# Batch 0 attended partly in front of the feed-forward and partly inside it, casts on GpSimd, weights cast by their transfers: windowed attention and a gated feed-forward in one kernel

## The chip, the cores and the metric

The kernel runs on one core of a Trainium2 chip. The metric is the device time of one execution in microseconds (us); lower is better. The engines are TensorE (PE, with its weight loads as PEld), VectorE (DVE), ScalarE (ACT), GpSimd (POOL) and SyncE (SP), which issues all transfers of the kernel before.

## What is computed

```python
# q, k, v: (B, H, S, D) = (4, 8, 768, 64) float32; n_sink = 4, window = 128
scores = q @ k^T / sqrt(D)
keep = (key position < 4) | (0 <= query position - key position < 128)
a = softmax over keys of the kept scores
x = (a @ v), heads side by side: (3072, 512)
out = (max(x @ w_gate, 0) * (x @ w_val)) @ w_out     # w_gate, w_val: 512 x 1536; w_out: 1536 x 512
```

## The kernel before

A *unit* is two heads of one batch; `U` holds 16 units, four to a batch (`NP` = 4). Its work is a row of six *stages*: `T(u)` transposes k and q on PE and copies them out of PSUM into `kE` (ACT) and `qT` (DVE); `Sg(u, g)`, for g = 0 to 2, makes the scores of a group of key blocks on PE and their exp on ACT into `ee`; `V(u, part)`, for two halves of the sequence, multiplies by v and by ones on PE and divides on DVE (two 32x32 transposes, a reciprocal, a product) into `xT`. The mask comes in one of two ways: with `bias=True` a matmul adds it (L199), otherwise DVE multiplies the exp by `msk` (L209).

Ahead of the stages stand the loads on SP's queue, `load_kq` (L89) and `load_v` (L94), and the casts from float32 to bf16, `cast_qk` (L110) and `cast_v` (L103). `cast_v` also copies the first four rows of v into three places (L108).

The feed-forward runs in *chunks*: `chunk(b, g, m)` (L235) makes 128 of the 1,536 hidden columns (m of 12) for half g of batch b: four matmuls with `wg` (L242), relu on ACT (L245), four with `wv` (L247), a product on DVE into `hT` (L249). It needs `xT` of all four units of the batch for its half. `ffn2(b, t, m)` (L256) is the second layer, 12 matmuls for each 128 rows, then a copy on ACT and a store from SP.

The order is written out by hand, and each engine and queue takes its instructions in the order of the program. Batch 0 is attended first, all four units with their three groups and both halves (L285 to L306). The weights come through a float32 staging buffer `wst` and are cast on GpSimd (L114 to L131, called from L291 to L312). Then 96 *slots* follow, one chunk each, 24 to a batch; in the slots of a batch the stages of the next batch's units are placed:

```python
slots = [(0, g, m) for m in range(FM) for g in range(2)]
...
want.append(max(0, s - 11) * 2)                      # slots 0 to 23: stages placed after slot s
...
want.append(min(len(stages), 24 + (s - 23)))         # later slots: one stage each
```

So the 24 stages of batch 1 lie in slots 12 to 23, two to a slot, and from slot 24 on each slot holds one stage. From slot 24 on up to three `ffn2` matmuls are taken in each slot from a queue (L356). Units 4 to 6 are loaded before the slots, a later unit three units ahead, when its forerunner's T comes (L317).

PSUM: `PP` is a pair of two-bank tiles that T, Sg and V take in turn; inside the slots T takes both, one for k and one for q (L177). `G` are four single banks; a chunk takes two of the first three in rotation.

Of the kernel before, what the change touches and what calls it, by code (L numbers as in the profile page):

```python
# [19 lines left out]
def kernel(  # L20
# [28 lines left out]
    NQ, NV, NW, NE, NT = 3, 3, 3, 3, 3  # L49
# [9 lines left out]
    wst = [const.tile([128, 2048], F32, name=f"wst{i}") for i in range(NW)]  # L59
# [43 lines left out]
    def cast_v(u, eng):  # L103
        src, dst = vf[u.i % NV], vn[u.i % NV]
        eng.tensor_copy(dst[:].rearrange("p j h d -> p (j h d)"), src[:].rearrange("p j h d -> p (j h d)"))  # L105
        o = dst[0:4, 1:7, :, :].rearrange("p (i e) h d -> p i e (h d)", e=2)[:, :, 0, :]
        s = src[0:4, 0, :, :].rearrange("p h d -> p (h d)").unsqueeze(1).to_broadcast([4, 3, 128])
        eng.tensor_copy(o, s)  # L108

    def cast_qk(u, ke, qe):  # L110
        for eng, src, dst in ((ke, kf[u.i % NQ], kn[u.i % 2]), (qe, qf[u.i % NQ], qn[u.i % 2])):
            eng.tensor_copy(dst[0:PR], src[0:PR].rearrange("p h (n d) -> p n h d", d=64))  # L112

    def load_w(c, w, dst, i, o):  # L114
        n = 256
        nc.sync.dma_start(out=wst[i % NW][:, o:o + KO * n].rearrange("p (ko n) -> p ko n", n=n),
                          in_=w.rearrange("(ko ki) n -> ki ko n", ki=128)[:, :, c * n:(c + 1) * n])

    def cast_w(c, dst, i, o, eng):
        n = 256  # L120
        eng.tensor_copy(dst[:, :, c * n:(c + 1) * n],
                        wst[i % NW][:, o:o + KO * n].rearrange("p (ko n) -> p ko n", n=n))

    def load_wo(c, i):
        nc.sync.dma_start(out=wst[i % NW][:].rearrange("p (ko n) -> p ko n", n=d_model),
                          in_=moe_w_out.rearrange("(ko ki) n -> ki ko n", ki=128)[:, 4 * c:4 * c + 4, :])

    def cast_wo(c, i, eng):
        for h in range(2):
            eng.tensor_copy(wo[:, 4 * c + 2 * h:4 * c + 2 * h + 2, :].rearrange("p ko n -> p (ko n)"),  # L130
                            wst[i % NW][:, 1024 * h:1024 * h + 1024])  # L131
# [137 lines left out]
    with tc.manual_schedule():  # L269
        for i in range(NV):  # L270
            nc.vector.memset(vf[i][:, 6, :, :], 0.0)
        for u in U[0:3]:
            load_kq(u)
            if u.p:
                load_v(U[u.p - 1])
        setup()

        def head_T(u):
            cast_qk(u, nc.gpsimd, nc.vector)
            T(u)  # L280

        head_T(U[0])
        load_kq(U[3])
        load_v(U[2])
        for p in range(NP):  # L285
            if p + 1 < NP:
                head_T(U[p + 1])
            for g in range(3):
                Sg(U[p], g, bias=True)
            cast_v(U[p], nc.gpsimd)  # L290
            if p == 0:  # L291
                load_v(U[3])
                for c in range(3):
                    load_w(c, moe_w_gate, wg, c, 0)
                    load_w(c, moe_w_val, wv, c, 1024)
            if p >= 1:
                for part in range(2):
                    V(U[p - 1], part)
        for c in range(6):
            cast_w(c, wg, c, 0, nc.gpsimd)  # L300
            cast_w(c, wv, c, 1024, nc.gpsimd)
            if c + 3 < 6:
                load_w(c + 3, moe_w_gate, wg, c + 3, 0)
                load_w(c + 3, moe_w_val, wv, c + 3, 1024)
        for part in range(2):
            V(U[3], part)  # L306
        for u in U[4:7]:
            load_kq(u)
            load_v(u)
        for c in range(3):  # L310
            load_wo(c, c)
            cast_wo(c, c, nc.gpsimd)  # L312

        head[0] = False
        stages = []

        def first(i):  # L317
            cast_qk(U[i], nc.gpsimd, nc.gpsimd)
            cast_v(U[i], nc.gpsimd)
            T(U[i])  # L320
            if i + 3 < len(U):
                load_kq(U[i + 3])
                load_v(U[i + 3])

        def stage_T(i):
            return lambda: first(i)

        n_u = len(U)
        order = []
        for i in range(NP, n_u):  # L330
            order.append(stage_T(i))
            order += [lambda i=i, g=g: Sg(U[i], g) for g in range(3)]
            order += [lambda i=i, part=part: V(U[i], part) for part in range(2)]

        stages = order
        slots = [(0, g, m) for m in range(FM) for g in range(2)]
        for b in range(1, B):
            slots += [(b, g, m) for g in range(2) for m in range(FM)]
        want = []
        for s in range(len(slots)):  # L340
            if s < 24:
                want.append(max(0, s - 11) * 2)
            else:
                want.append(min(len(stages), 24 + (s - 23)))
        f2 = deque()
        si = 0
        for s, (b, g, m) in enumerate(slots):
            if s % 24 == 0:
                while si < min(len(stages), 24 * b):
                    stages[si]()  # L350
                    si += 1
            chunk(b, g, m)
            while si < want[s]:
                stages[si]()
                si += 1
# [46 lines left out]
```

## Time and profile before

| | us |
|---|---|
| median of 3 runs | 309.78 (308.88 to 309.84) |
| the profiled execution | 308.14 |
| its span in the profile | 306.4 |

The span is what the profile covers from its first to its last instruction; 1.74 us of the profiled execution lie around it. A page cuts the span into 40 slices of 7.66 us and gives each engine's busy share in tenths. Times in the rows are counted from the span's start. "Idle before" is the time in which the engine had nothing to do before the instruction, with what ended it.

### The profile page before, as it was taken

The numbers are of one execution on the slowest core, as the hardware profiler recorded it, in microseconds if no ns is written. First come the engines' busy times: TensorE is split into PE (matmuls) and PEld (weight loads), VectorE is DVE, ScalarE is ACT, GpSimd is POOL, SyncE is SP. The second block draws the span as 40 slices with busy tenths as digits, with TensorE's granted clock in tenths as the row PEclk, the third lists the DMA queues.
The fourth block names the chain that finished last, engine by engine and source line by source line (L and its number), as shares of the span: only waits on it lengthen the run. The fifth ranks groups of instructions, "written<-read, shape, count | busy, mean of one in ns | idle before, by whom it ended". The sixth has DMA issues, their size and how long they took to land.

```text
span 306.4 us, 5389 instructions
## 1 busy us (share of the span) xinstructions
PE 264.9 (86%) x2114; PEld 147.6 (48%) x2136; DVE 160.2 (52%) x300; ACT 123.6 (40%) x250; POOL 72.7 (24%) x90
## 2 busy tenths in 40 slices
PE   1868659908796977999999999999999999999995
PEld 1343435504444544555555555555555555555442
DVE  5453953403947767575757575757575622222100
ACT  3464303304343453545454545454535233333221
POOL 5457640189424044040404040400000000000000
PEclk9995989965958999999999999999999999999999
DMA  7999999939972300150446044000000000000022
GB/s 197 241 249 348 349 253 230 335 128 232 233 162 69 89 0 2 51 141 37 130 104 148 37 127 99 0 36 34 37 0 36 34 36 34 35 36 34 34 103 103
DMA packets 44104, 35.13 MB, mean 115 GB/s; under 512 B 27184, under 2 KB 33328, under 8 KB 44080
## 3 DMA queue, kind: packets, MB, share of 16 engines
q1 hardware_dynamic: 44080, 34.81, 43.8%
q8 instruction: 16, 0.26, 0.4%
q14 instruction: 8, 0.07, 0.1%
HBM read 28.51 MB, written 6.29 MB: 114 GB/s over the span
## 4 chain that ended last, share of the span: by engine, by line
PE 71%; DVE 10%; DMA 8%; SPq 3%; ACT 2%; issue 2%; POOL 2%; DVEq 0%; ACTq 0%; POOLq 0%
PE g L262 18%; PE g L242 17%; PE g L247 17%; PE pp L203 5%; PE pp L220 4%; PE pp L262 3%; DMA wst<-in_moe_w_out_dram 3%; DMA vf<-in_v_dram 3%; PE pp L180 2%; PE pp L199 2%; DMA qf<-in_q_dram 2%; ACT ee L207 2%; DVE R L228 2%; DVE xT L230 2%; DVE t L226 2%
## 5 line engine op out<-in xcount | busy, mean ns | idle before, releaser
L249 DVE TENSOR_TENSOR hT<-gs,g 128x384 bf16<-128x384 f32 x96 | 53.1, 553 | 68.2 <-PE g L247 67.3
L245 ACT ACTIVATE gs<-g 128x384 f32<-128x384 f32 x96 | 47.2, 491 | 98.4 <-PE g L242 88.3
L242 PE MATMUL g<-xT,wg 128*128 128x384 bf16 x384 | 82.2, 338 | 4.1 <-DVE xT L230 4.1
L247 PE MATMUL g<-xT,wv 128*128 128x384 bf16 x384 | 81.6, 337 | 0.0
L262 PE MATMUL g<-wo,hT 128*128 128x512 bf16 x218 | 61.0, 381 | 1.6 <-issue 0.6
L207 ACT ACTIVATE ee<-pp 128x1006 bf16<-128x1006 f32 (+2 forms) x48 | 45.4, 959 | 32.6 <-PE pp L203 32.5
L242 PEld LDWEIGHTS <-wg 128*128 128x128 bf16 x384 | 37.4, 100 | 37.4 <-issue 6.9
L247 PEld LDWEIGHTS <-wv 128*128 128x128 bf16 x384 | 38.8, 101 | 28.6 <-issue 5.2
L209 DVE TENSOR_TENSOR ee<-ee,msk 128x1006 bf16<-128x1006 bf16 (+2 forms) x36 | 25.2, 703 | 26.9 <-ACT ee L207 26.7
L112 POOL CAST kn<-kf 96x1024 bf16<-96x1024 f32 x16 | 16.6, 1036 | 89.9 <-PE pp L180 62.4
L262 PEld LDWEIGHTS <-hT 128*128 128x128 bf16 x288 | 24.5, 98 | 24.8 <-issue 3.3
L203 PE MATMUL pp<-qT,kE 64*128 64x251 bf16 (+4 forms) x224 | 20.1, 282 | 4.6 <-DVE qT L185 4.6
L228 DVE STREAM_TRANSPOSE R<-r 128x384 f32<-128x384 f32 x32 | 18.5, 579 | 1.1
L203 PEld LDWEIGHTS <-kE 64*128 64x128 bf16 x224 | 8.1, 100 | 22.5 <-issue 17.2
L266 ACT COPY ot<-g 128x512 f32<-128x512 f32 x20 | 11.7, 583 | 15.8 <-PE g L262 15.8
L220 PEld LDWEIGHTS <-vn 128*64 128x64 bf16 x288 | 12.8, 110 | 10.0 <-issue 8.9
L105 POOL CAST vn<-vf 128x896 bf16<-128x896 f32 x16 | 15.0, 940 | 8.6 <-DMA vf<-in_v_dram 8.6
L180 PEld LDWEIGHTS <-kn 96*128 96x128 bf16 x128 | 7.9, 107 | 18.9 <-POOL kn L112 14.8
L185 DVE COPY qT<-pp 128x768 bf16<-128x768 bf16 x12 | 11.5, 957 | 9.6 <-PE pp L180 8.7
L226 DVE STREAM_TRANSPOSE t<-pp 128x384 f32<-128x384 f32 x24 | 13.9, 579 | 2.5 <-PE pp L220 1.7
L230 DVE TENSOR_TENSOR xT<-pp,R 128x384 bf16<-128x384 f32 x24 | 13.4, 557 | 0.8
L180 PE MATMUL pp<-ident,kn 96*128 96x96 bf16 x96 | 6.4, 211 | 8.1 <-POOL kn L112 7.5
(55 smaller groups left out, 183.5 us busy)
## 6 DMA issues: line engine op xcount, KB each, us to landing
kf<-in_k_dram SPq DMA_DIRECT2D x16, 384.0 KB
qf<-in_q_dram SPq DMA_DIRECT2D x16, 384.0 KB
vf<-in_v_dram SPq DMA_DIRECT2D x32, 192.0 KB
out_dram<-ot SPq DMA_DIRECT2D x24, 256.0 KB
wst<-in_moe_w_gate_dram SPq DMA_DIRECT2D x6, 512.0 KB
wst<-in_moe_w_val_dram SPq DMA_DIRECT2D x6, 512.0 KB
wst<-in_moe_w_out_dram SPq DMA_DIRECT2D x3, 1024.0 KB
vf<-in_v_dram SPq DMA_DIRECT2D x16, 12.0 KB
```

The source lines that it names most:

```text
L180: nc.tensor.transpose(ps.bitcast(BF16)[:, 96 * n:96 * n + 96], x[0:PR, n, :, :].rearrange("p h d -> p (h d)"), ident[0:PR, 0:PR])
L203: nc.tensor.matmul(out=ps[:, h, c0:c1], lhsT=kE[t][64 * h:64 * h + 64, x0:x0 + 128], rhs=qT[t][64 * h:64 * h + 64, q0:q0 + c1 - c0], start ...
L207: nc.scalar.activation(x, ps[:, :, 0:n], Act.Exp, bias=0.0, scale=scale)
L209: nc.vector.tensor_tensor(x, x, msk[:, g, 0:n].unsqueeze(1).to_broadcast([128, 2, n]), op=Alu.mult)
L220: nc.tensor.matmul(out=(pv, pd)[which][64 * h:64 * h + 64, o0:o0 + c1 - c0], lhsT=w, rhs=ee[u.i % NE][:, g, h, c0:c1], start=i == 0, stop= ...
L226: nc.vector.transpose(out=t1[:], in_=pd[:, 0:CUT])
L228: nc.vector.transpose(out=R[:].rearrange("p (c e) -> p c e", e=32), in_=r[:].unsqueeze(2).to_broadcast([128, CUT // 32, 32]))
L242: nc.tensor.matmul(out=gp[:, 0:CUT], lhsT=wg[:, ko, m * 128:(m + 1) * 128], rhs=x[:, ko, c], start=ko == 0, stop=ko == KO - 1)
L245: nc.scalar.activation(gs[:], gp[:, 0:CUT], Act.Relu, bias=0.0, scale=1.0)
L247: nc.tensor.matmul(out=vp[:, 0:CUT], lhsT=wv[:, ko, m * 128:(m + 1) * 128], rhs=x[:, ko, c], start=ko == 0, stop=ko == KO - 1)
L249: nc.vector.tensor_tensor(h[:, m, c], gs[:], vp[:, 0:CUT], op=Alu.mult)
L262: nc.tensor.matmul(out=op, lhsT=hT[b % 2][:, m, t * 128:(t + 1) * 128], rhs=wo[:, m, :], start=m == 0, stop=m == FM - 1)
```

## The change

The order of batch 0 is new. Before the slots stand T of its four units, the first two score groups and the first V half of each, and the third group of units 0 and 1. The rest (the third group of units 2 and 3, the second V half of each) goes into slots 0 to 5, one stage to a slot. Slots 0 to 5 are chunks 0 to 5 of the first half, slots 6 to 11 the same chunks of the second half, and then the halves alternate as before. The 24 stages of batch 1 lie in slots 6 to 23, four to three slots; from slot 24 on everything stands in the slots of before.

`T` no longer brings its casts along: `front(i)` issues casts and loads four slots ahead of T, and loads one unit ahead. All casts of q and k are on GpSimd; the row copies of `cast_v` are on ACT for batch 0. `gate(u)` writes two elements of the unit's `kf` on GpSimd, so that SP's load of that unit waits until GpSimd's queue has come to that point.

The staging buffer and its casts are gone. `load_w(m0, m1)` and `load_wo(c)` are transfers that GpSimd issues and that convert from float32 to bf16 on the way, eight for `wg` and `wv` (two of 256 columns and two of 512 for each) and three for `wo`. `kE`, `qT`, `ee`, `vf` and `vn` get four buffers instead of three.

```diff
--- before.py
+++ after.py
@@ -46,7 +46,7 @@
     npool = ctx.enter_context(tc.tile_pool(name="np", bufs=2))
     pspool = ctx.enter_context(tc.tile_pool(name="ps", bufs=1, space=bass.MemoryType.PSUM))
 
-    NQ, NV, NW, NE, NT = 3, 3, 3, 3, 3
+    NQ, NV, NE, NT = 3, 4, 4, 4
     kf = [const.tile([128, 2, 512], F32, name=f"kf{i}") for i in range(NQ)]
     qf = [const.tile([128, 2, 512], F32, name=f"qf{i}") for i in range(NQ)]
     vf = [const.tile([128, 7, 2, 64], F32, name=f"vf{i}") for i in range(NV)]
@@ -56,7 +56,6 @@
     ee = [const.tile([128, 3, 2, 512], BF16, name=f"ee{i}") for i in range(NE)]
     qn = [const.tile([128, NR, 2, 64], BF16, name=f"qn{i}") for i in range(2)]
     kn = [const.tile([128, NR, 2, 64], BF16, name=f"kn{i}") for i in range(2)]
-    wst = [const.tile([128, 2048], F32, name=f"wst{i}") for i in range(NW)]
     wg = const.tile([128, KO, d_ff], BF16, name="wg")
     wv = const.tile([128, KO, d_ff], BF16, name="wv")
     wo = const.tile([128, FM, d_model], BF16, name="wo")
@@ -100,35 +99,28 @@
         nc.sync.dma_start(out=dst[0:24, 6, :, :],
                           in_=v[u.b, 2 * u.p:2 * u.p + 2, 744:768, :].rearrange("h s d -> s h d"))
 
-    def cast_v(u, eng):
+    def cast_v(u, sinks):
         src, dst = vf[u.i % NV], vn[u.i % NV]
-        eng.tensor_copy(dst[:].rearrange("p j h d -> p (j h d)"), src[:].rearrange("p j h d -> p (j h d)"))
+        nc.gpsimd.tensor_copy(dst[:].rearrange("p j h d -> p (j h d)"), src[:].rearrange("p j h d -> p (j h d)"))
         o = dst[0:4, 1:7, :, :].rearrange("p (i e) h d -> p i e (h d)", e=2)[:, :, 0, :]
-        s = src[0:4, 0, :, :].rearrange("p h d -> p (h d)").unsqueeze(1).to_broadcast([4, 3, 128])
-        eng.tensor_copy(o, s)
-
-    def cast_qk(u, ke, qe):
-        for eng, src, dst in ((ke, kf[u.i % NQ], kn[u.i % 2]), (qe, qf[u.i % NQ], qn[u.i % 2])):
-            eng.tensor_copy(dst[0:PR], src[0:PR].rearrange("p h (n d) -> p n h d", d=64))
-
-    def load_w(c, w, dst, i, o):
-        n = 256
-        nc.sync.dma_start(out=wst[i % NW][:, o:o + KO * n].rearrange("p (ko n) -> p ko n", n=n),
-                          in_=w.rearrange("(ko ki) n -> ki ko n", ki=128)[:, :, c * n:(c + 1) * n])
-
-    def cast_w(c, dst, i, o, eng):
-        n = 256
-        eng.tensor_copy(dst[:, :, c * n:(c + 1) * n],
-                        wst[i % NW][:, o:o + KO * n].rearrange("p (ko n) -> p ko n", n=n))
-
-    def load_wo(c, i):
-        nc.sync.dma_start(out=wst[i % NW][:].rearrange("p (ko n) -> p ko n", n=d_model),
-                          in_=moe_w_out.rearrange("(ko ki) n -> ki ko n", ki=128)[:, 4 * c:4 * c + 4, :])
-
-    def cast_wo(c, i, eng):
-        for h in range(2):
-            eng.tensor_copy(wo[:, 4 * c + 2 * h:4 * c + 2 * h + 2, :].rearrange("p ko n -> p (ko n)"),
-                            wst[i % NW][:, 1024 * h:1024 * h + 1024])
+        sinks(o, src[0:4, 0, :, :].rearrange("p h d -> p (h d)").unsqueeze(1).to_broadcast([4, 3, 128]))
+
+    def cast_kq(u):
+        for src, dst in ((kf[u.i % NQ], kn[u.i % 2]), (qf[u.i % NQ], qn[u.i % 2])):
+            nc.gpsimd.tensor_copy(dst[0:PR], src[0:PR].rearrange("p h (n d) -> p n h d", d=64))
+
+    def gate(u):
+
+        nc.gpsimd.memset(kf[u.i % NQ][0:1, 0, 0:2], 0.0)
+
+    def load_w(m0, m1):
+        for w, dst in ((moe_w_gate, wg), (moe_w_val, wv)):
+            nc.gpsimd.dma_start(out=dst[:, :, m0 * 128:m1 * 128],
+                                in_=w.rearrange("(ko ki) n -> ki ko n", ki=128)[:, :, m0 * 128:m1 * 128])
+
+    def load_wo(c):
+        nc.gpsimd.dma_start(out=wo[:, 4 * c:4 * c + 4, :],
+                            in_=moe_w_out.rearrange("(ko ki) n -> ki ko n", ki=128)[:, 4 * c:4 * c + 4, :])
 
     def setup():
         nc.vector.memset(warm[:], 0.0)
@@ -269,98 +261,108 @@
     with tc.manual_schedule():
         for i in range(NV):
             nc.vector.memset(vf[i][:, 6, :, :], 0.0)
-        for u in U[0:3]:
-            load_kq(u)
-            if u.p:
-                load_v(U[u.p - 1])
+        for i, what in ((0, load_kq), (1, load_kq), (2, load_kq), (0, load_v)):
+            what(U[i])
         setup()
-
-        def head_T(u):
-            cast_qk(u, nc.gpsimd, nc.vector)
-            T(u)
-
-        head_T(U[0])
+        gp_copy, act_copy = nc.gpsimd.tensor_copy, nc.scalar.copy
+        cast_kq(U[0])
+        T(U[0])
+        cast_kq(U[1])
+        T(U[1])
         load_kq(U[3])
-        load_v(U[2])
-        for p in range(NP):
-            if p + 1 < NP:
-                head_T(U[p + 1])
-            for g in range(3):
-                Sg(U[p], g, bias=True)
-            cast_v(U[p], nc.gpsimd)
-            if p == 0:
-                load_v(U[3])
+        for u in U[1:4]:
+            load_v(u)
+        Sg(U[0], 0, bias=True)
+        cast_kq(U[2])
+        Sg(U[0], 1, bias=True)
+        cast_v(U[0], act_copy)
+        T(U[2])
+        Sg(U[1], 0, bias=True)
+        cast_kq(U[3])
+        Sg(U[1], 1, bias=True)
+        load_w(0, 2)
+        V(U[0], 0)
+        cast_v(U[1], act_copy)
+        T(U[3])
+        load_w(2, 4)
+        Sg(U[2], 0, bias=True)
+        Sg(U[2], 1, bias=True)
+        V(U[1], 0)
+        cast_v(U[2], act_copy)
+        gate(U[4])
+        load_kq(U[4])
+        load_v(U[4])
+        Sg(U[3], 0, bias=True)
+        Sg(U[3], 1, bias=True)
+        V(U[2], 0)
+        cast_v(U[3], act_copy)
+        load_w(4, 8)
+        Sg(U[0], 2, bias=True)
+        V(U[3], 0)
+        Sg(U[1], 2, bias=True)
+        head[0] = False
+
+        def prep(i):
+            cast_kq(U[i])
+            cast_v(U[i], gp_copy)
+
+        def load(i):
+            if i < len(U):
+                load_kq(U[i])
+                load_v(U[i])
+
+        def front(i):
+
+            prep(i)
+            if i == 4:
+                gate(U[5])
+                load(5)
+                load_w(8, 12)
+            elif i == 5:
+                gate(U[6])
+                load(6)
                 for c in range(3):
-                    load_w(c, moe_w_gate, wg, c, 0)
-                    load_w(c, moe_w_val, wv, c, 1024)
-            if p >= 1:
-                for part in range(2):
-                    V(U[p - 1], part)
-        for c in range(6):
-            cast_w(c, wg, c, 0, nc.gpsimd)
-            cast_w(c, wv, c, 1024, nc.gpsimd)
-            if c + 3 < 6:
-                load_w(c + 3, moe_w_gate, wg, c + 3, 0)
-                load_w(c + 3, moe_w_val, wv, c + 3, 1024)
-        for part in range(2):
-            V(U[3], part)
-        for u in U[4:7]:
-            load_kq(u)
-            load_v(u)
-        for c in range(3):
-            load_wo(c, c)
-            cast_wo(c, c, nc.gpsimd)
-
-        head[0] = False
-        stages = []
-
-        def first(i):
-            cast_qk(U[i], nc.gpsimd, nc.gpsimd)
-            cast_v(U[i], nc.gpsimd)
-            T(U[i])
-            if i + 3 < len(U):
-                load_kq(U[i + 3])
-                load_v(U[i + 3])
-
-        def stage_T(i):
-            return lambda: first(i)
-
-        n_u = len(U)
-        order = []
-        for i in range(NP, n_u):
-            order.append(stage_T(i))
-            order += [lambda i=i, g=g: Sg(U[i], g) for g in range(3)]
-            order += [lambda i=i, part=part: V(U[i], part) for part in range(2)]
-
-        stages = order
-        slots = [(0, g, m) for m in range(FM) for g in range(2)]
+                    load_wo(c)
+            else:
+                load(i + 1)
+
+        f2 = deque()
+        slots = [(0, 0, m) for m in range(6)] + [(0, 1, m) for m in range(6)]
+        slots += [(0, g, m) for m in range(6, FM) for g in range(2)]
         for b in range(1, B):
             slots += [(b, g, m) for g in range(2) for m in range(FM)]
-        want = []
-        for s in range(len(slots)):
-            if s < 24:
-                want.append(max(0, s - 11) * 2)
-            else:
-                want.append(min(len(stages), 24 + (s - 23)))
-        f2 = deque()
-        si = 0
+        plan = [[] for _ in slots]
+        first = [("V", 0, 1), ("S", 2, 2), ("V", 1, 1), ("S", 3, 2), ("V", 2, 1), ("V", 3, 1)]
+        for s, x in enumerate(first):
+            plan[s].append(x)
+        later = []
+        for i in range(NP, len(U)):
+            later += [("T", i, 0)] + [("S", i, g) for g in range(3)] + [("V", i, 0), ("V", i, 1)]
+        for x, st in enumerate(later):
+            plan[6 + x * 18 // 24 if x < 24 else x].append(st)
+        pre = [[] for _ in slots]
+        for s, p in enumerate(plan):
+            for st in p:
+                if st[0] == "T":
+                    pre[max(0, s - 4)].append(st[1])
         for s, (b, g, m) in enumerate(slots):
-            if s % 24 == 0:
-                while si < min(len(stages), 24 * b):
-                    stages[si]()
-                    si += 1
+            for i in pre[s]:
+                front(i)
             chunk(b, g, m)
-            while si < want[s]:
-                stages[si]()
-                si += 1
+            for what, i, x in plan[s]:
+                if what == "T":
+                    T(U[i])
+                elif what == "S":
+                    Sg(U[i], x, bias=i < NP)
+                else:
+                    V(U[i], x)
             for _ in range(3):
                 if f2:
                     f2.popleft()()
-            if b == 0 and s == 23:
+            if s == 23:
                 f2 += [lambda t=t, mm=mm: ffn2(0, t, mm) for t in range(6) for mm in range(FM)]
             if b > 0 and m == FM - 1:
                 f2 += [lambda b=b, t=t, mm=mm: ffn2(b, t, mm) for t in range(3 * g, 3 * g + 3) for mm in range(FM)]
-        assert si == len(stages)
         tail[0] = 1
         while f2:
             f2.popleft()()
```

## Rows read from the trace of the kernel before

**Rows 1.** The page: PE's busy tenths in 40 slices, and the transfer queue.
```profile
PE   1868659908796977999999999999999999999995
...
q1 hardware_dynamic: 44080, 34.81, 43.8%
```

**Rows 2.** Busy time by stretch (first line: the columns).
```profile
core 0: us, PE busy (x) PEld busy (x) DVE busy (x) ACT busy (x) POOL busy (x), PEclk, DMA share, GB/s
0.00:42.36 42.36, 25.12 (x289) 14.09 (x290) 25.11 (x60) 16.99 (x34) 24.21 (x35) 0.92 1.08 277
61.10:68.61 7.51, 0.00 (x0) 0.01 (x1) 0.55 (x1) 0.00 (x0) 6.26 (x8) 0.66 0.38 139
81.39:94.29 12.90, 10.28 (x91) 5.67 (x90) 8.30 (x16) 5.30 (x11) 3.44 (x4) 0.74 0.73 146
106.39:119.96 13.57, 9.18 (x108) 5.92 (x109) 10.73 (x21) 6.18 (x16) 4.89 (x6) 1.00 0.01 1
119.96:306.40 186.44, 181.20 (x1345) 99.83 (x1364) 93.28 (x167) 78.26 (x154) 18.93 (x23) 1.00 0.20 60
```

**Rows 3.** Timeline: start, duration, engine, instruction; in brackets the idle time before it.
```profile
14.30 0.69 DVE L112 CAST qn<-qf 96x1024 bf16<-96x1024 f32 x1 [2.39 <-DMA qf<-in_q_dram]
...
23.98 1.16 POOL L105 CAST vn<-vf 128x896 bf16<-128x896 f32 x1 [1.55 <-DMA vf<-in_v_dram]
...
42.36 0.81 PE L242 MATMUL g<-xT,wg 128*128 128x384 bf16 x4 [3.02 <-DVE xT L230]
...
108.35 0.50 PE L180 MATMUL pp<-ident,qn 96*128 96x96 bf16 x8 [1.46 <-DVE xT L230]
...
110.00 0.39 PE L203 MATMUL pp<-qT,kE 64*128 64x255 bf16 x4 [1.14 <-DVE qT L185]
```

**Rows 4.** Waits: total us, times, longest.
```profile
POOL wo L130 <- DMA wst<-in_moe_w_out_dram: 17.3, 3, 16.1
```

**Rows 5.** The chain that ended last: start, duration, what.
```profile
72.16 1.39 PE g L242 x4
...
124.12 0.75 PE g L262 x3
...
128.52 0.71 PE pp L220 x16
...
130.63 0.65 PE g L247 x4
131.28 0.83 PE pp L220 x20
...
143.89 0.71 PE pp L220 x16
```

**Rows 6.** Timeline of DVE, one unit and one mask product earlier.
```profile
73.24 1.12 DVE L209 TENSOR_TENSOR ee<-ee,msk 128x1006 bf16<-128x1006 bf16 x1 [1.83 <-ACT ee L207]
...
108.89 0.96 DVE L185 COPY qT<-pp 128x768 bf16<-128x768 bf16 x1
...
111.47 0.69 DVE L209 TENSOR_TENSOR ee<-ee,msk 128x1006 bf16<-128x1006 bf16 x1 [1.62 <-ACT ee L207]
...
114.45 0.55 DVE L249 TENSOR_TENSOR hT<-gs,g 128x384 bf16<-128x384 f32 x1
114.92 0.58 DVE L226 STREAM_TRANSPOSE t<-pp 128x384 f32<-128x384 f32 x1
...
116.88 0.57 DVE L226 STREAM_TRANSPOSE t<-pp 128x384 f32<-128x384 f32 x1
```

**Rows 7.** Groups by line: busy us, mean ns of one, idle before.
```profile
L207 ACT ACTIVATE ee<-pp 128x1006 bf16<-128x1006 f32 (+2 forms) x48 | 45.4, 959 | 32.6 <-PE pp L203 32.5
...
L112 POOL CAST qn<-qf 96x1024 bf16<-96x1024 f32 x12 | 12.4, 1032 | 2.9 <-PE pp L180 1.8 <-DMA vf<-in_v_dram 0.9
...
L108 POOL CAST vn<-vf 4x384 bf16<-4x384 f32 x16 | 8.6, 539 | 1.0
...
L112 DVE CAST qn<-qf 96x1024 bf16<-96x1024 f32 x4 | 2.7, 685 | 2.7 <-DMA qf<-in_q_dram 2.7
```

**Rows 8.** SP's issues of w_out: duration in ns, shortest, median, longest.
```profile
L125 SPq DMA_DIRECT2D wst<-in_moe_w_out_dram x3: 458/1037/2275, 52.1 to 55.7; - x3
```

## The prediction

> **What bounds the kernel now.** I read the page first, for which engine is full and when; then the busy times by stretch, to cut the span where its character changes; then the timeline and the waits, for what the idle time waits for; then the chain that ended last, for the pace of the good part.
>
> The page shows TensorE (PE) nearly full in the last 24 slices and patchy before [rows 1]. I cut at the first feed-forward chunk (42.36), at the transposes of unit 4 (68.61) and at the chunk of slot 25 (119.96) [rows 2]. From 119.96 to the end PE is busy 181.2 of 186.4 us at a granted clock of 1.00 (2.4 GHz): that part is bound by PE, and only less PE work would shorten it. The 120 us in front of it are not bound by PE. So the change is judged by one number: when slot 25 starts.
>
> Three things fill those 120 us. Until 42.36, attention of batch 0 runs alone, transfers move 277 GB/s on full DMA engines (share 1.08) [rows 2], and the first chunk ends a 3.02 us wait for the last xT, since all four units with both halves come first [rows 3]. From 61.1 to 68.61 PE does nothing [rows 2]: unit 4's casts stand behind those of w_out in GpSimd's queue, and these wait up to 16.1 us for their transfer [rows 4]. From 68.61 on, 24 attention stages lie in 12 slots. A unit with its three chunks takes 12.9 us [rows 2]; PE waits 1.46 us for a PSUM pair that VectorE (DVE) is still reading, then 1.14 us for the qT copy [rows 3].
>
> **Prices at the full clock.** From the chain in the steady part [rows 5]: a chunk 2 x 0.65 = 1.30, V 0.71 and 0.83 for its halves, three ffn2 matmuls 0.75. Six slots take 143.89 - 128.52 = 15.37 us, so the whole PE work of a unit is 15.37 - 6 x 1.30 - 6 x 0.75 = 3.07. On DVE [rows 6]: hT product 0.55, qT 0.96, a mask at most 0.69, a V half 116.88 - 114.92 = 1.96; a unit is 0.96 + 3 x 0.69 + 2 x 1.96 = 6.95.
>
> **The change, part by part.**
>
> *Behind slot 25: nothing.* Stages 24 to 71 keep their slots and their order on PE, ACT and DVE. Loads run one unit ahead instead of three, issued ten slots before use, which is 10 x 15.37 / 6 = 25 us at a DMA share of 0.20 [rows 2]; without that cover a T would be late, and V behind it. Casts only move earlier on a GpSimd that is busy 18.9 of 186.4 us [rows 2]. The 186.4 us stay.
>
> *Staging.* 18 weight casts leave GpSimd and 15 weight issues leave SP. Four q casts move from DVE (0.685) to GpSimd (1.03) [rows 7], 0.35 us each, hidden in the wait for loads. Four row copies move from GpSimd (0.54) [rows 7] to ACT; I keep 0.5 for each, an estimate.
>
> *Eleven casting transfers in GpSimd's queue.* No row has one. Let X be GpSimd's time for one. Below it is nothing; above I take SP's longest weight issue, 2.28 us [rows 8], by the ratio of GpSimd to DVE in the q cast (1.5): 3.4. I take 2.5, towards the upper end, since here the engine itself writes out 512 row pairs.
>
> *Start of slot 0.* Loads now come as kq 0 to 2, v0, kq3, v1 to v3. Before, kq 0 to 2 and v0 had landed at 14.3, where the third q cast's wait for its load ends [rows 3]. kq3 is 0.79 MB, at 0.277 MB/us 2.9 us: 17.2; its q cast ends at 18.4. Then GpSimd's queue sets the pace: two weight issues (2X), the v1 cast (0.9, as the 1.03 of a q cast with an eighth fewer columns), two more issues (2X), the v2 cast: 20.2 + 4X. Behind the v2 cast stand ACT's row copy (0.5), two exps of unit 3 (2 x 0.96 [rows 7]), its V (0.2 + 0.8) and the DVE chain with the rest of the V before it (2.1), less 0.4 for the three matmuls of a chunk that need only the other units. Slot 0 starts at 25.4 + 4X = 35.4.
> For X near nothing there is a floor: batch 0 and the first four weight blocks are 6.8 MB, 25 us at 0.277 from a start at 2, and from the last v its cast, copy, V and DVE chain (0.9 + 0.5 + 0.8 + 2.0): 31. Before, v3 had landed at 24.0 [rows 3].
> All transfers of before stand in one queue row [rows 1], so no row shows two in competition. The Trainium skill, page "DMA: Bandwidth & Descriptors", section "Queues, rings and completion order", says that a DMA engine alternates between its queue rows packet by packet. By that, v3 slips behind weights to about 30 and slot 0 starts at 34 to 36 whatever X is; by the row it stays at 24 and the floor above holds.
>
> *Slots 0 to 5.* Six chunks 7.8, four V halves 3.3, two biased score groups 1.6 (an estimate: 3.07 less V and transposes, a third of it, doubled for the bias): 12.7. Slot 6 needs the last V half through DVE (1.96): 14.65. The weights for slots 4 to 7 are issued at 31 to 36; 2.1 MB beside unit 4's 1.2 MB land by 44. Slot 4 starts at 35.4 + 2 (clock, below) + 8.5 = 46: hidden, by little.
>
> *Slots 6 to 23.* 18 chunks and 24 stages: PE 18 x 1.30 + 4 x 3.07 = 35.7; DVE 18 x 0.55 + 4 x 6.95 = 37.7. Neither is reached, because both work in order. I laid the slot list out by hand with the prices above: a T with S in the same slot (6, 15) waits 1.25 for qT; a T behind two V halves of one slot waits 1.7 for the PSUM pair (10, 19), behind halves in two slots 1.25 (15, 24); V behind two scores of one slot 0.4 (13, 22). Slots 6 to 14: 17.8 + 1.25 + 1.7 + 0.4 = 21.2; slots 15 to 23: the same and 1.25: 22.4. Slot 24 with chunk, T, its wait and ffn2: 4.0. Together 47.6.
>
> *Masks beside casts.* A mask took 1.12 us while GpSimd cast, 0.69 otherwise [rows 6]. Casts of four units (4 x 3.5 us) lie in a stretch of 44 us, so about a third of 12 masks: 4 x 0.43 = 1.7, half of it on the path: 1.
> The skill's page "SBUF — State Buffer", section "Who interferes with whom", says that a DVE instruction with two SBUF inputs and a GpSimd instruction that reads SBUF shut each other out for a whole instruction. The trace agrees (0.69 to 1.12); were all 12 masks caught, the sum would be 5 us longer instead of 1.
>
> *Clock.* Behind an idle stretch PE runs at the lower level (1.2 GHz): four matmuls take 1.39 us at 72.16, 0.65 later [rows 5]. The time before slot 0 stays patchy, so the first chunks and scores cost 2 us more, once. The hole before 68.61, behind which the clock stood at 0.66 to 0.74 [rows 2], has no counterpart.
>
> *Sum.* Slot 25: 35.4 + 14.65 + 47.6 + 1 + 2 = 100.7 against 119.96, 19 less. The span is 100.7 + 186.4 = 287.1; with the 1.74 us around the profiled span **289 us**. That execution (308.14) lies 1.6 below the median of 309.78, so it may be 290 in the median's terms; I keep 289.
>
> **The rivals.**
> 1. *GpSimd's queue becomes the bound* (slower than before). The casts of v1 to v3 stand behind weight issues; the price is 4X on slot 0. Slot 25 is back at 119.96 when 25.4 + 4X + 65.3 reaches it: X = 7.3 us. At X = 10 the time is 319. For: no row shows GpSimd issuing a transfer. Against: it casts 96x1024 in 1.03 us [rows 7] and SP issues the same rows in 2.28 at most [rows 8]. Chance 0.08.
> 2. *Casting transfers land slowly.* At half the rate seen (0.139 MB/us) the weights of slots 4 to 7 need 15 us and with unit 4's loads land at 51; slot 4 waits 5: 294. At a third, 58: 301. For: conversion on the way and 512-byte rows at the destination, which no row shows. Against: nothing but the 277 GB/s of plain weights and loads together. Chance 0.2.
> 3. *The clock stays low in slots 6 to 23.* Waits like those at T left the clock at 0.74 in one unit and at 1.00 in a later stretch [rows 2]. Four stretches of some 5 us cost up to 2 each: 297. Chance 0.15.
> 4. *Better than worked out*: slot 0 at its floor of 31 and half of T's waits gone: 279 to 284. Chance 0.1.
> 5. *Work moves and nothing is freed*: slots wait for the last weights or w_out. 18.9 MB must land by slot 24, 70 us at 0.277, against 97. Chance 0.02, 309.
>
> **Numbers.** The likeliest, 284 to 294, has 0.45. Rivals 2 and 3 reach to 305, rival 4 to 279: the range is 279 to 305 and leaves out rivals 1 and 5 and the tails. Faster by over 0.3% (about what a measurement of this kernel can tell from no change) 0.90, within 0.3% 0.02, slower 0.08.
>
> **What would show it.** First chunk at 34 to 38; slot 6 some 15 to 17 us later; no 7 us hole of PE; the chunk of slot 25 at 97 to 105 with 186 us behind it; GpSimd's gaps at the first weight issues give X. It is wrong if the v1 cast ends after 30, if slot 4 waits for weights, if the clock falls in slots 6 to 23, or if the part behind slot 25 grows because a load one unit ahead is late.

## The result and the profile after

The changed kernel takes 285.89 us (median of 4, 285.24 to 286.68), the kernel before, run beside it, 309.81 us (median of 4): a ratio of 0.9225 [0.9178, 0.9272]. The profiled execution took 286.49 us, its span 284.5 us, with 1.99 us around it. Ratios, here and below, leave out executions in a slower state of the chip; the times in us are medians of all.

The page of the kernel after, the two lines that answer to [rows 1], both transfer queues and the busy times:
```profile
PE 259.5 (91%) x2136; PEld 144.4 (51%) x2136; DVE 157.7 (55%) x298; ACT 124.2 (44%) x254; POOL 65.9 (23%) x86
...
PE   1797795979789899999999999999999999999994
PEclk9999997799799999999999999999999999999999
...
q1 hardware_dynamic: 36160, 25.37, 37.6%
q0 software_dynamic: 5808, 4.72, 10.5%
```
Behind the first slice, which is as before, the slices with little PE work in the first half of [rows 1] are gone but for one. In two places the granted clock is lower. Weights now have a queue row of their own (q0).

Busy times of the kernel after by stretch, cut at the first chunk, the chunk of slot 6 and the chunk of slot 25 (columns as in [rows 2]):
```profile
0.00:30.46 30.46, 18.35 (x192) 9.88 (x193) 15.21 (x42) 16.34 (x36) 19.71 (x32) 1.00 1.13 219
30.46:45.51 15.05, 13.67 (x147) 8.37 (x147) 10.22 (x22) 4.45 (x8) 4.94 (x8) 1.00 0.85 159
45.51:98.15 52.64, 44.73 (x433) 26.44 (x432) 38.08 (x69) 25.13 (x56) 21.48 (x26) 0.90 0.89 169
98.15:284.50 186.35, 182.75 (x1366) 99.69 (x1364) 94.21 (x167) 78.27 (x154) 19.74 (x23) 1.00 0.24 67
```
The cut at slot 6 needs a word: its chunk issues three matmuls at 43.47, waits, and ends the fourth at 46.32; 45.51 is where four in a row would begin that end there, so most of the wait counts to slots 0 to 5, as in the prediction.

Slot 25 starts at 98.15 instead of 119.96, 21.8 us earlier; behind it nothing changed (186.35 against 186.44). Of the 21.8, 42.36 - 30.46 = 11.9 lie ahead of the first chunk and 9.9 between it and slot 25.

Timeline of PE in the kernel after, the places where it waited:
```profile
30.46 0.81 PE L234 MATMUL g<-xT,wg 128*128 128x384 bf16 x4 [1.79 <-DVE xT L222]
...
46.00 0.32 PE L234 MATMUL g<-xT,wg 128*128 128x384 bf16 x1 [1.86 <-DVE xT L222]
...
49.70 0.60 PE L195 MATMUL pp<-qT,kE 64*128 64x255 bf16 x4 [1.14 <-DVE qT L177]
...
61.42 0.50 PE L172 MATMUL pp<-ident,qn 96*128 96x96 bf16 x8 [1.46 <-DVE xT L222]
...
72.60 0.50 PE L172 MATMUL pp<-ident,qn 96*128 96x96 bf16 x8 [0.96 <-DVE xT L222]
74.24 0.60 PE L195 MATMUL pp<-qT,kE 64*128 64x255 bf16 x4 [1.14 <-DVE qT L177]
...
```
The 7.5 us hole in front of unit 4 [rows 2] has no counterpart. Waits like those in [rows 3] remain: unit 4 waits for qT (1.14), unit 5 for a PSUM pair (1.46), unit 6 for both (0.96 and 1.14); units 7 and 8 wait for the pair again (1.46 and 0.96).

Timeline of GpSimd in the kernel after, its first weight transfers:
```profile
17.80 1.04 POOL L110 CAST qn<-qf 96x1024 bf16<-96x1024 f32 x1 [0.47 <-DMA qf<-in_q_dram]
18.78 0.88 POOL L118 DMA_DIRECT2D wg<-in_moe_w_gate_dram  x1
19.65 0.76 POOL L118 DMA_DIRECT2D wv<-in_moe_w_val_dram  x1
20.39 0.96 POOL L104 CAST vn<-vf 128x896 bf16<-128x896 f32 x1
...
24.14 0.93 POOL L104 CAST vn<-vf 128x896 bf16<-128x896 f32 x1 [0.42 <-DVE R L220]
```
A casting transfer holds GpSimd for about 0.75 us. The last line is the cast of v3; the profile puts the 0.42 us of waiting in front of it down to VectorE, not to its load.

### The profile page after: what moved, and what is told of

Same layout as the page of the kernel before. It is cut to its first block, busy times and chain, and to the rows that moved or that the text cites. A ratio compares the mean times of both kernels' runs of the same rounds, so it can differ in the third digit from the quotient of the medians.

```text
span 284.5 us, 5389 instructions
## 1 busy us (share of the span) xinstructions
PE 259.5 (91%) x2136; PEld 144.4 (51%) x2136; DVE 157.7 (55%) x298; ACT 124.2 (44%) x254; POOL 65.9 (23%) x86
## 4 chain that ended last, share of the span: by engine, by line
PE 77%; DVE 10%; DMA 5%; ACT 3%; issue 3%; POOL 1%; SPq 0%; POOLq 0%; DVEq 0%; ACTq 0%
PE g L234 20%; PE g L239 20%; PE g L254 20%; DMA qf<-in_q_dram 5%; PE pp L212 5%; PE pp L195 4%; PE pp L254 4%; PE pp L172 3%; DVE R L220 2%; DVE t L218 2%; ACT ee L199 2%; DVE xT L222 2%; DVE hT L241 2%; DVE r L219 1%; DVE qT L177 1%
## 5 line engine op out<-in xcount | busy, mean ns | idle before, releaser
L234 PE MATMUL g<-xT,wg 128*128 128x384 bf16 x384 | 79.8, 331 | 3.7 <-DVE xT L222 3.7
L239 PE MATMUL g<-xT,wv 128*128 128x384 bf16 x384 | 79.7, 331 | 0.0
L254 PE MATMUL g<-wo,hT 128*128 128x512 bf16 x240 | 64.3, 381 | 0.0
L234 PEld LDWEIGHTS <-wg 128*128 128x128 bf16 x384 | 35.8, 98 | 34.3 <-issue 4.3
L201 DVE TENSOR_TENSOR ee<-ee,msk 128x1006 bf16<-128x1006 bf16 (+2 forms) x36 | 25.9, 718 | 24.7 <-ACT ee L199 24.5
L195 PE MATMUL pp<-qT,kE 64*128 64x251 bf16 (+4 forms) x224 | 18.9, 263 | 2.3 <-DVE qT L177 2.3
L110 POOL CAST qn<-qf 96x1024 bf16<-96x1024 f32 x16 | 17.0, 1064 | 10.3 <-DMA qf<-in_q_dram 6.8
L218 DVE STREAM_TRANSPOSE t<-pp 128x384 f32<-128x384 f32 x28 | 16.2, 580 | 3.0 <-PE pp L212 2.1
L222 DVE TENSOR_TENSOR xT<-pp,R 128x384 bf16<-128x384 f32 x28 | 15.6, 557 | 1.0
L212 PE MATMUL pp<-ee,vn 128*64 128x251 bf16 (+8 forms) x256 | 14.4, 238 | 0.0
L212 PE MATMUL pp<-ee,ones 128*64 128x251 bf16 (+8 forms) x256 | 13.7, 233 | 0.0
## 6 DMA issues: line engine op xcount, KB each, us to landing
wv<-in_moe_w_val_dram POOLq DMA_DIRECT2D x2, 512.0 KB, 11.9
```

The costliest lines, as they stand in the source:

```text
L110: nc.gpsimd.tensor_copy(dst[0:PR], src[0:PR].rearrange("p h (n d) -> p n h d", d=64))
L195: nc.tensor.matmul(out=ps[:, h, c0:c1], lhsT=kE[t][64 * h:64 * h + 64, x0:x0 + 128], rhs=qT[t][64 * h:64 * h + 64, q0:q0 + c1 - c0], start ...
L201: nc.vector.tensor_tensor(x, x, msk[:, g, 0:n].unsqueeze(1).to_broadcast([128, 2, n]), op=Alu.mult)
L212: nc.tensor.matmul(out=(pv, pd)[which][64 * h:64 * h + 64, o0:o0 + c1 - c0], lhsT=w, rhs=ee[u.i % NE][:, g, h, c0:c1], start=i == 0, stop= ...
L218: nc.vector.transpose(out=t1[:], in_=pd[:, 0:CUT])
L234: nc.tensor.matmul(out=gp[:, 0:CUT], lhsT=wg[:, ko, m * 128:(m + 1) * 128], rhs=x[:, ko, c], start=ko == 0, stop=ko == KO - 1)
```

## The experiments

My theory was that GpSimd's queue, which works in order, held the kernel before back: the casts of staged weights in it wait for transfers, and casts of attention stand behind them. Casting transfers remove these waits, and the new order fills the slots with work. The rivals: one of the two parts does it alone; or the split of batch 0 does.

**The two parts alone (e1, e2).** e1 is the kernel before with its weights loaded by casting transfers at the places of its old loads; e2 is the kernel after with its weights staged through SP again (the staging lies in `hT[1]`, which is not in use then).

Of e1:
```diff
-        nc.sync.dma_start(out=wst[i % NW][:, o:o + KO * n].rearrange("p (ko n) -> p ko n", n=n),
+        nc.gpsimd.dma_start(out=dst[:, :, c * n:(c + 1) * n],
...
-            cast_w(c, wg, c, 0, nc.gpsimd)
-            cast_w(c, wv, c, 1024, nc.gpsimd)
```
Of e2:
```diff
-            nc.gpsimd.dma_start(out=dst[:, :, m0 * 128:m1 * 128],
...
+                nc.sync.dma_start(out=x, in_=w.rearrange("(ko ki) n -> ki ko n", ki=128)[:, :, m * 128:m * 128 + 256])
...
+                nc.gpsimd.tensor_copy(dst[:, :, m * 128:m * 128 + 256], x)
```


> The kernel before with one part of the change: all weights come by casting transfers from GpSimd at the places of its old weight loads; the order of the stages stays. Theory A (the order is what cost the 120 us in front of slot 25): the first chunk stays near 42 us, the 7.5 us hole in front of unit 4 goes, and 1 to 2 us of the lower clock behind it; the time falls from 309.8 to some 299 to 302. Theory B (the staging held the kernel back, and the order follows from it): first chunk at 36 or earlier, 288 to 293.

> The changed kernel with its order, but with weights loaded by SP into a float32 staging buffer of two blocks (it lies in hT of batch 1, which is free until slot 24) and cast on GpSimd at the places where the casting transfers stood. Theory A: the order keeps most of the gain; GpSimd waits for each weight block in front of the casts of v1 to v3, so the first chunk moves from 30.5 to about 40, the rest stays: 293 to 297. Theory B: the order is worth little without casting transfers: 303 or more.

e1: 302.56 us, ratio 0.9781 [0.9707, 0.9856]; e2: 306.02, 0.99 [0.9834, 0.9966]. Alone they bring 7 and 4 us, together 24. e1 comes near the time of theory A, but its first chunk moves as neither theory had it; e2 comes out as theory B had it. Timeline of GpSimd in e1, the casts of v2 and v3:
```profile
26.91 0.94 POOL L104 CAST vn<-vf 128x896 bf16<-128x896 f32 x1 [5.36 <-DMA vf<-in_v_dram]
...
34.53 0.94 POOL L104 CAST vn<-vf 128x896 bf16<-128x896 f32 x1 [6.12 <-DMA vf<-in_v_dram]
```
In e1 the hole in front of unit 4 is gone: from the first chunk to slot 25 it takes 112.27 - 47.19 = 65.1 us instead of 119.96 - 42.36 = 77.6. But the first chunk moves from 42.36 to 47.19: six weight transfers leave GpSimd from 13.07 on and run beside the loads, and v3 is cast at 34.5 instead of 24.0 [rows 3]. That is what the rule of the Trainium skill that a DMA engine alternates between its queue rows (page "DMA: Bandwidth & Descriptors", section "Queues, rings and completion order") would make of it; the runs show the delay, not the packets. In the kernel after, where the first weight transfer leaves at 18.78, v3 is cast at 24.14, and not at about 30 as the prediction worked out by that rule.

Timeline of GpSimd in e2, the casts of w_out and behind them those of unit 6:
```profile
81.28 2.02 POOL L137 CAST wo<-hT 128x1024 bf16<-128x1024 f32 x2 [10.96 <-DMA hT<-in_moe_w_out_dram]
...
89.05 2.03 POOL L137 CAST wo<-hT 128x1024 bf16<-128x1024 f32 x2 [3.14 <-DMA hT<-in_moe_w_out_dram]
91.02 1.03 POOL L110 CAST kn<-kf 96x1024 bf16<-96x1024 f32 x1
```
e2's first chunk comes at 39.11, as worked out (40), but the old hole is back in a new place, in front of unit 6. Timeline of PE in e2:
```profile
92.10 0.82 PE L187 MATMUL pp<-ident,kn 96*128 96x96 bf16 x8 [12.12 <-POOL kn L110]
```
w_out's casts wait for their loads, unit 6 stands behind them, and slot 25 starts at 119.17. I had not followed GpSimd's queue so far, and missed by 9 us. So in these two forms neither part does it alone: the order needs a GpSimd that does not wait. e2 issues each load right in front of its cast and has two staging blocks instead of three, so a part of its waits may be its own; staged loads issued earlier were not tried with the new order.

**The spread and the split (e3, e4).** e3 puts batch 1's stages two to a slot in slots 12 to 23, as before; e4 attends batch 0 wholly in front.

Of e3:
```diff
-            plan[6 + x * 18 // 24 if x < 24 else x].append(st)
+            plan[12 + x // 2 if x < 24 else x].append(st)
```
Of e4, ahead of slot 0 and in the plan:
```diff
+        V(U[0], 1)
+        Sg(U[2], 2, bias=True)
+        V(U[1], 1)
+        Sg(U[3], 2, bias=True)
+        V(U[2], 1)
+        V(U[3], 1)
...
-        first = [("V", 0, 1), ("S", 2, 2), ("V", 1, 1), ("S", 3, 2), ("V", 2, 1), ("V", 3, 1)]
+        first = []
```


> The changed kernel with the 24 stages of batch 1 in slots 12 to 23, two to a slot as before, in place of four to three slots from slot 6 on. Theory A: slots 6 to 11 then hold chunks alone (7.8 us) and four units take the 12.1 us of before each: 56 us instead of 52.7, so 289 to 290. If the spread is the larger part of the gain: 294 or more. If it is of no use: 286.

> The changed kernel with batch 0 attended wholly in front of slot 0 (two score groups and four V halves more there, none in slots 0 to 5). Theory A': the split is worth little by itself, because the four V halves need 7.8 us of DVE in either place: first chunk at 38 to 39, slots 0 to 5 take 7.8 instead of 15.0, slot 6 without its 1.9 us wait: 285 to 288. Rival: chunks beside V halves hide them, the split is worth its 7 to 8 us: 292 to 294.

e3: 294.0, 0.9505 [0.9423, 0.9587]; e4: 286.07, 0.9247 [0.9184, 0.931]. Busy times of e3 from the chunk of slot 6 to that of slot 25, cut at 55.15 where the stages begin:
```profile
47.35:55.15 7.80, 7.31 (x46) 4.40 (x46) 3.20 (x6) 2.91 (x6) 3.65 (x6) 1.00 0.54 111
55.15:106.36 51.21, 39.99 (x387) 23.37 (x387) 34.98 (x63) 22.42 (x51) 15.55 (x18) 0.83 0.72 137
```
These are 59.0 us against the 52.64 of the kernel after. Of the 6.4 between them PE's busy time makes 2.6 (47.30 and 44.73; the clock is 0.83) and its idle time 3.8. The time is 8 us longer, not the 3 to 4 that I expected; the rest lies ahead of slot 0 (32.31 and 30.46), which the edit does not touch. By itself the split is worth nothing that the intervals could tell: e4's first chunk is 7.4 us later, but six slots follow in 9.5 us instead of 15.05, and slot 25 starts at 95.97. What was taken out of the head was only put into the slots.

**The price of an issue (e5).** Each transfer of `wg` and `wv` goes out in four quarters.
```diff
-            nc.gpsimd.dma_start(out=dst[:, :, m0 * 128:m1 * 128],
...
+            for o in range(4):
+                nc.gpsimd.dma_start(out=dst[:, o:o + 1, m0 * 128:m1 * 128],
...
```


> The changed kernel with each transfer of w_gate and w_val cut in four (one for each 128 rows of the weight), the same bytes and row lengths: 32 issues for them instead of 8. In the profile one issue took GpSimd 0.75 us. If that is a fixed price of an issue, a block costs 3.0 instead of 0.75 each, the first chunk moves by up to 4 x 2.25 = 9 us (from 30.5 to 38 or 39.5) and the time to 293 to 295; this is the price of rival 1 of the prediction. If the price goes with the number of rows, nothing moves: 286.

290.9, 0.9369 [0.9313, 0.9426]. The line's group in e5 (count; shortest, median, longest ns) and one block in its timeline:
```profile
L119 POOL DMA_DIRECT2D wg<-in_moe_w_gate_dram x16: 533/605/679, 19.2 to 46.2; - x16
```
```profile
19.24 2.29 POOL L119 DMA_DIRECT2D wg<-in_moe_w_gate_dram  x4
```
The same group in the kernel after, with its time to landing:
```profile
L118 POOL DMA_DIRECT2D wg<-in_moe_w_gate_dram x4: 740/754/881, 18.8 to 40.5; - x4
...
DMA to landing us min/median/max: 6.3/9.0/12.8
```
A quarter costs 0.605, the whole 0.754: most of the price is per issue. A block takes 2.29 instead of 0.75, and the first chunk starts at 35.57, 5.1 us later, where the prediction's 4X gives 4 x 1.54 = 6.2. So the queue does set the pace there; X was small. The time lies between my two forecasts, since a quarter costs 0.605 and not the whole's 0.75.

**The gate (e8).** `gate(u)` issues nothing.
```diff
-        nc.gpsimd.memset(kf[u.i % NQ][0:1, 0, 0:2], 0.0)
+        pass
```


> The changed kernel without the two-element writes that hold SP's loads of units 4 to 6 until GpSimd has issued weights: those loads go out as soon as their buffers are free. If loads and weight transfers share the engines packet by packet (in the run with casting transfers alone the first chunk moved from 42.4 to 47.2 when weights went out at 13 us beside the loads), the weights of slots 0 to 7 land later, and slot 0 or slot 4 waits: 287 to 291. If there is room for both: 285 to 286.

286.41, 0.9223 [0.9169, 0.9276]: no difference. But its profile answers another question. Busy times of e8 from slot 6 to slot 25, and PE's wait at slot 6:
```profile
47.32:95.68 48.36, 40.65 (x432) 25.04 (x432) 36.79 (x69) 24.92 (x56) 16.97 (x21) 1.00 0.81 152
```
```profile
47.81 0.32 PE L234 MATMUL g<-xT,wg 128*128 128x384 bf16 x1 [1.84 <-DVE xT L222]
```
At a granted clock of 1.00 the stretch takes 48.36, where I had predicted 48.6; in the kernel after, at 0.90, 52.64. From slot 0 to slot 25 PE is idle for 9.28 us in both profiles, and busy for 54.49 in e8 and 58.41 in the kernel after: the 3.9 us between them are clock. The wait at slot 6 (1.84 and 1.86) stands in both, so it alone does not decide.

**The waits inside the slots (e6, e7, e12, e9).** e6 puts eight chunks of the first half first; e7 gives T one pair for k and q together; e12 does so with the `kE` copies ahead of the `qT` copy; e9 puts q of units 4 to 7 into the fourth single bank, which chunks do not use until `ffn2`.
Of e6:
```diff
-        slots = [(0, 0, m) for m in range(6)] + [(0, 1, m) for m in range(6)]
-        slots += [(0, g, m) for m in range(6, FM) for g in range(2)]
+        slots = [(0, 0, m) for m in range(8)] + [(0, 1, m) for m in range(8)]
+        slots += [(0, g, m) for m in range(8, FM) for g in range(2)]
```
Of e7 and e12, and below of e9:
```diff
-        tk, tq = two() if head[0] else (pair()[:, 0, :], pair()[:, 0, :])
+        tk, tq = two()
```
```diff
-        tk, tq = two() if head[0] else (pair()[:, 0, :], pair()[:, 0, :])
+        tk, tq = two() if head[0] else (pair()[:, 0, :], G[3][:] if u.b == 1 else pair()[:, 0, :])
```


> The changed kernel with chunks 0 to 7 of the first half in slots 0 to 7, those of the second half in 8 to 15, then alternating; the stages keep their slots. The last V half of batch 0 (slot 5) is then needed in slot 8. Theory A (the wait at slot 6 is a matter of order, and the lower clock behind it follows from it): the 1.86 us wait goes and up to 2.7 us of lower clock at 46 to 53: 281 to 284. Rival (DVE's chain sets the pace there and the next T waits for it): the wait moves on to slot 6's T: 285 to 286.

> The changed kernel with T's k and q in the two banks of one PSUM pair in place of one bank of each pair, so that T waits for one V half's reader only. Theory P (the PSUM pair is what T waits for): the waits of 1.46, 0.96, 1.46 and 0.96 us before qn in slots 10, 15, 19 and 24 go: 281 to 283. Theory D (DVE works in order, its copy of qT stands behind the V halves in any case): S waits for qT by what T no longer waits: 285 to 286.

> The changed kernel with T's k and q in one pair and with ACT's kE copies placed ahead of DVE's qT copy in the program. If the order of the two readers of a pair was what cost 5 us with one pair, the cost goes: kE is copied while DVE still works on the V halves, and qT is copied when DVE would have come to it anyway: 284 to 286 under theory D, 281 to 283 under theory P. If any shared pair costs: 289 or more.

> The changed kernel with T's q of units 4 to 7 in the single bank G3, which nothing uses before slot 24; k stays in a bank of a pair. T then waits for one V half's reader only, and k and q stay in different tiles (with both in one pair ACT's kE copies waited for DVE's qT copy, 28 us in all, and the time rose to 291.6). Theory P (the PSUM pair is what T waits for): the waits of 1.46 us go, 282 to 284. Theory D (DVE's order decides): S waits for qT as before, 285 to 286.

| | us | ratio |
|---|---|---|
| e6 | 284.13 | 0.9142 [0.9082, 0.9202] |
| e7 | 291.6 | 0.9376 [0.9311, 0.944] |
| e12 | 287.24 | 0.9242 [0.919, 0.9294] |
| e9 | 282.48 | 0.9095 [0.9044, 0.9145] |

e6 takes away the wait at slot 6, and a wait of 0.70 us for the pair appears at T in that slot; its gain, 1.8 us by the medians, is not clear, since the intervals overlap. e7 was to save a pair and lost 5 us by the ratios. The waits of e7 (total us, times, longest), and its timeline at unit 5:
```profile
ACT kE L178 <- DVE qT L177: 28.0, 12, 3.8
```
```profile
60.71 0.27 ACT L178 COPY kE<-pp 128x128 bf16<-128x128 bf16 x1 [3.41 <-DVE qT L177]
...
61.03 0.28 PE L195 MATMUL pp<-qT,kE 64*128 64x255 bf16 x2 [1.45 <-ACT kE L178]
```
Both copies only read, each its own bank, yet ACT's waits for DVE's: the copies of one pair tile come one after the other, in the order of the program. e12 turns the order round, and 4 us come back; now DVE's copy waits for ACT's (8 times, 9.2 us). I had taken it that sharing a pair costs nothing. That was wrong for e7's order; in e12's the price, if there is one, is too small to tell (0.9242 against 0.9225). With two pairs, as in the kernel after, no copy of T waits for the other.

e9 has a bank of its own for q. Its timeline of PE and the busy times from slot 6 to slot 25:
```profile
60.59 0.39 PE L195 MATMUL pp<-qT,kE 64*128 64x255 bf16 x4 [1.14 <-DVE qT L177]
...
71.36 0.39 PE L195 MATMUL pp<-qT,kE 64*128 64x255 bf16 x4 [1.95 <-DVE qT L177]
```
```profile
46.02:93.38 47.36, 40.42 (x432) 25.18 (x433) 37.19 (x69) 24.75 (x56) 20.90 (x25) 1.00 0.98 180
```
The waits of 1.46 at T are gone, and S waits for qT instead: 1.14 in unit 5, 1.95 in unit 6. Against e8, also at clock 1.00, the stretch is one us shorter (47.36, 48.36). The rest of its difference to the 52.64 of the kernel after is clock. So the time is the one forecast for theory P, but most of what T no longer waits S waits for qT, as in theory D. Of e9's gain in time, 3.4 us, the trace ties about one to the edit.

**The head, and all together (e10, e11).** e10 is e6 with T of unit 3 and the cast of v1 ahead of the first weight issues; e11 adds e9's bank.
```diff
-        load_w(0, 2)
+        T(U[3])
         V(U[0], 0)
         cast_v(U[1], act_copy)
-        T(U[3])
+        load_w(0, 2)
         load_w(2, 4)
```


> The changed kernel with chunks 0 to 7 of the first half first, and in front of slot 0 unit 3's T and the v1 cast ahead of the first weight issues. If the chain in front of slot 0 runs through those two issues (1.6 us) and through ACT's wait of 2.4 us for the v1 cast, as the chain of the changed kernel shows: first chunk at 28 to 29, 281 to 283. If v's loads or the weights set it instead: 284, as with eight chunks alone.

> The changed kernel with all three mends: eight chunks of the first half first, unit 3's T and the v1 cast ahead of the first weight issues, and q of units 4 to 7 transposed into the free bank. If the three waits are separate places on one chain, their sizes add: slot 0 at 29.3, no wait for xT up to slot 24, slots 6 to 24 in 47.4: slot 25 at 90 to 92, 278 to 280. If DVE's order gives back what one mend frees: 281 to 283.

e10's ratio, 0.9055 [0.8974, 0.9135], rests on two of its six executions (280.31 and 283.1 us); the median of all six is 284.6, and its profile is of one of 284.64. So e10 is not settled. e11 takes 281.8, 0.9098 [0.9073, 0.9124]. Both profiles start the first chunk at 29.3; with the head unchanged it starts at 29.5 (e9) to 32.3 (e3), so up to a us or two of the head may be theirs. But e11's slot 25 starts at 93.26, e9's at 93.38: in the time the mends do not add up.

The rival had it that DVE's order gives back what one mend frees. PE's time from slot 0 to slot 25, parted into busy and idle, says something else (the work is the same, so at one clock the busy time would be about the same in all rows):

| | us | busy | idle |
|---|---|---|---|
| kernel after | 67.69 | 58.41 | 9.28 |
| e8 | 63.77 | 54.49 | 9.28 |
| e6 | 65.08 | 56.23 | 8.85 |
| e9 | 63.92 | 55.60 | 8.32 |
| e10 | 66.97 | 57.72 | 9.25 |
| e11 | 63.96 | 57.13 | 6.83 |

e11 idles 1.5 us less than e9, and is busy 1.5 us longer for the same work: what it gained went to the clock in that profile (0.95 over these slots, 0.97 in e9's). From slot 1 to slot 23 its PE waits for no xT, and waits for qT instead. Timeline of PE in e11:
```profile
47.74 0.39 PE L195 MATMUL pp<-qT,kE 64*128 64x255 bf16 x4 [1.69 <-DVE qT L177]
...
69.88 0.39 PE L195 MATMUL pp<-qT,kE 64*128 64x255 bf16 x4 [1.82 <-DVE qT L177]
```
So DVE gives back a part, not all. e9 and e11 beat both kernels, as their intervals lie below that of the kernel after; between the two nothing is shown.

## Why the prediction was right

The time, 285.89, lies 3.1 below the 289.0 forecast, inside 284 to 294. But two of its terms were off by more than that and cancelled, so that it came so near is in part luck.

| term | predicted | profile after |
|---|---|---|
| X, GpSimd's time for one casting transfer | 2.5 | 0.75 |
| start of slot 0 | 35.4 | 30.46 |
| slots 0 to 5 (with the wait at slot 6) | 14.65 and 2 (clock) | 15.05 |
| slots 6 to 24 | 47.6 and 1 (masks) | 52.64 |
| behind slot 25 | 186.4 | 186.35 |
| span | 287.1 | 284.5 |

*Start of slot 0: mis-sized by X.* The bounds 0 to 3.4 held the 0.75; I went to the upper end since 512 row pairs are much to write, and e5 shows that their number hardly counts. With 0.75, 25.4 + 4X is 28.4. The chain that ended last, ahead of slot 0 in the kernel after:
```profile
9.57 8.07 DMA qf<-in_q_dram
17.80 1.04 POOL qn L110
...
20.39 0.97 POOL vn L104
...
21.38 0.51 ACT vn L106
...
22.83 0.91 ACT ee L199
...
30.46 0.81 PE g L234 x4
```
kq3 lands at 17.65 (predicted 17.2), and the way leads through its q cast, two weight issues and the v1 cast as I had it. Then it leaves GpSimd: ACT's row copy of v1 waits for the cast, and behind it stand the `kE` copies of unit 3 and the exps of units 2 and 3. This queue I had entered behind v2 only; the chain puts most of the 2 us between 28.4 and 30.46 there, though the same head starts between 29.46 (e9) and 32.31 (e3) in other profiles. The floor of 31 was no floor: the kernel after starts at 30.46, with v3 cast at 24.14, and e9 to e11 start at 29.3 to 29.5.

*Slots 0 to 5: right*, but the 2 us of clock did not come: the clock was 1.00. In e4, e6, e9 and e11 it stood at 0.82 to 0.90 in the first slots, so the term comes in some runs and not in others.

*Slots 6 to 23: the waits right, the clock as in rival 3.* Predicted waits were 1.96 at slot 6 (1.86), 1.25 for qT (1.14), 1.7 and 1.25 for the pair (1.46 and 0.96); the 0.4 in front of V did not show. At clock 1.00 the stretch takes 48.36 and 48.63 (e8, e4), as predicted. The profiled run had 0.90 there: 4 us, of rival 3's 8. In the chain of that run four matmuls took 1.40 us at 50.31 and at 74.84, and 0.65 at 61.92. These are two stretches of the kind that the rival names, each behind two short waits (1.86 and 1.14; 0.96 and 1.14). What lets the clock fall stays open: e8 had the same wait at slot 6 and kept 1.00.

*Masks: little.* 36 masks took 25.2 us before and 25.9 after; a us was allowed for.

*Rivals.* GpSimd as the bound (1) fell with X at 0.75. Slow landing (2) fell: `wg` and `wv` landed 6.3 to 12.8 us after their issue, and slot 4 waited for no weights. That nothing is freed (5) fell. The floor of rival 4 was reached, its shorter waits were not; the loss of rival 3 took that back.

## What to carry to other kernels

When an engine that works in order both starts things and waits for them, its waits are paid by whatever stands behind (unit 6 in e2, 12 us). One of two changes may then be worth little without the other: e1 and e2 alone bring 7 and 4 us, together 24. Follow each such queue to the end of the stretch, behind the first cast as well; and cut a forecast at places where one term can be checked against the trace, since two errors of 5 and 4 us hid behind a total that was 3 off. Here, moving work from in front of a stretch into it gained nothing by itself (e4), and evening it out inside did (e3). Before you call an edit of a few us a gain, part the time into busy and idle: between profiles of the same work the clock alone made up to 4 us.

## What the runs showed of the hardware

A transfer that converts float32 to bf16 takes GpSimd about 0.75 us, and 0.6 for a quarter of the rows. Copies by ACT and DVE out of different banks of one PSUM tile waited for each other (12 times in e7, 28.0 us); whether the chip or the program's semaphores, set for each tile, make them wait was not tried. The granted clock of the same stretch of work was 0.90 in one profile and 1.00 in others, worth 4 us, with the same waits ahead of it and the same idle time of PE (9.28 us from slot 0 to slot 25); the cause stays open.
